# A pruned-weight matmul whose first tokens are loaded ahead of its weights

## The chip, the cores and the metric

The kernel runs on one core of one Trainium2 chip. The metric is the device time of one execution in microseconds (us), as a median over executions. Time points in the text count from the start of the profiled span.

## The reference

```python
B, S, D = 16, 512, 1024            # x: [16, 512, 1024], w: [1024, 1024], b: [1024], bf16
N, M = 2, 4
wg = w.reshape(D // M, M, D)       # groups of four rows
mag = jnp.abs(wg)
order = jnp.argsort(mag, 1)
thr = jnp.take_along_axis(mag, order[:, M - N:M - N + 1, :], 1)
wp = (wg * (mag >= thr)).reshape(D, D)
return jnp.einsum("bsd,df->bsf", x, wp) + b
```

In each column, of every four weights in successive rows only those stay whose size is at least the second largest of the four. Then 8192 tokens are multiplied with the pruned matrix and the bias is added.

## The kernel before

**Weights.** A weight tile `w_gh[(g, h)]` holds half g of the rows and half h of the columns: 128 partitions with one group of four rows each (index m), 512 columns. They are pruned in six pieces; piece 0 is rows g = 0, columns 0 to 255. `load_w` (L69, its DMA at L71) loads a piece or two of its four rows.

VectorE prunes a piece in `abs_piece` (L109) and `prep_piece` (L124). With `abs` the sizes of the four rows, it forms `hi` and `lo`, the larger and smaller of each pair of rows; t1, the smaller `hi`; t2, the larger `lo`; and the threshold `thr`, the larger of t1 and t2, which is the second largest of four. `keep` compares the sizes with it (L150), `prune` multiplies the weights with the mask, in place (L153). In piece 0 the abs step goes by pairs of rows (m = 0, 1 and m = 2, 3), `hi` too, `lo` in one instruction. Then rows 0 and 1 are kept and pruned in two column halves each, and after them rows 2 and 3.

**Tokens.** 64 tiles of 128 tokens. For tiles 0 to 7, the first half of the features is loaded as it lies (`load_x`, L76, DMA at L79), transposed by TensorE (`transpose_half`, L182, four 128 x 128 transposes a tile into a PSUM bank) and copied to `xT` by ScalarE (`copy_half`, L187). Everything else is transposed by DMA.

**Queues.** Loads are issued from SP's DMA queue (q1 in the profile) and from ScalarE's (q10). Both run on the same 16 DMA engines. On ScalarE the two loads stand ahead of its activation table load.

**Order.** `K` keeps instructions in the order in which they are written. The start is written out by hand in the list `FRONT` (L285), read token by token. W and w are fillers on TensorE: matmuls of ones into an unused bank, 512 or 128 columns wide (`warm`, L105). T.t transposes tile t, C.t copies it. A.i and P.i are `abs_piece` and `prep_piece`. N.i.t.m is the product of tile t with row m of weight piece i (L203, 256 columns), M.i.t the same for all four rows. So N.0.0.0 is TensorE's first use of pruned weights and N.0.0.2 the first of rows 2 and 3. I, D, G, Q, L issue loads, U moves pruned weights from their group layout to `wp_nat`, V and O handle partial sums; the rest of the run is a loop over token tiles (L369).

Of the kernel before, what the change touches and what calls it, by code (L numbers as in the profile page):

```python
# [10 lines left out]
def kernel(  # L11
# [7 lines left out]
    nc = tc.nc  # L19
    P = 128  # L20
    bf16 = mybir.dt.bfloat16
    fp32 = mybir.dt.float32
    u16 = mybir.dt.uint16
    Alu = mybir.AluOpType
    Act = mybir.ActivationFunctionType
    K = tc.keep_in_program_order

    B, S, D = x.shape
# [10 lines left out]
    T, F = 8, 6  # L39
# [25 lines left out]
    def w_of(i):  # L65
        g, c0, c1 = pieces[i]
        return w_gh[(g, c0 // FH)][:, :, c0 % FH:c0 % FH + c1 - c0]

    def load_w(g, c0, c1, eng=nc.sync, m0=0, m1=4):  # L69
        dst = w_gh[(g, c0 // FH)][:, m0:m1, c0 % FH:c0 % FH + c1 - c0]  # L70
        K(eng.dma_start(dst, wv[:, g, m0:m1, c0:c1]))  # L71
# [4 lines left out]
    def load_x(ta, tb, eng=nc.sync):  # L76
        xt = const.tile([P, tb - ta, KH], bf16, name=f"xh_{ta}")
        src = xf[ta * P:tb * P, 0:KH].rearrange("(t p) c -> p t c", p=P)
        K(eng.dma_start(xt[:], src))  # L79
        for t in range(ta, tb):  # L80
            xh[t] = xt[:, t - ta, :]

    load_w(0, 0, 256, nc.sync, 0, 2)
    load_w(0, 0, 256, nc.scalar, 2, 4)
    load_x(0, 2)
    load_x(2, 4, nc.scalar)
    load_x(4, 5)
    load_x(5, 6)
    load_w(0, 256, 512)
# [16 lines left out]

    mags = {}

    def abs_piece(i, on_act):  # L109
        g, c0, c1 = pieces[i]  # L110
        n = c1 - c0
        if n <= 256:
            mag = mags_pool.tile([P, 4, n], bf16, name="mag")[:]
        else:
            mag = mag2_pool.tile([P, 4, n], bf16, name="mag2")[:]
        if on_act:
            K(nc.scalar.activation(mag, w_of(i), Act.Abs))
        else:
            for ms in (slice(0, 2), slice(2, 4)) if i == 0 else (slice(0, 4),):
                K(nc.vector.tensor_single_scalar(  # L120
                    mag[:, ms].bitcast(u16), w_of(i)[:, ms].bitcast(u16), 0x7FFF, op=Alu.bitwise_and))
        mags[i] = mag

    def prep_piece(i):  # L124
        g, c0, c1 = pieces[i]
        n = c1 - c0
        mag = mags.pop(i)
        magv = mag.rearrange("p (a j) f -> p a j f", j=2)
        hi = tmp.tile([P, 2, FH], bf16, name="hi")[:, :, :n]
        lo = tmp.tile([P, 2, FH], bf16, name="lo")[:, :, :n]  # L130
        for a in ((0, 1), (1, 2)) if i == 0 else ((0, 2),):
            a = slice(*a)
            K(nc.vector.tensor_tensor(hi[:, a], magv[:, a, 0, :], magv[:, a, 1, :], op=Alu.max))
        K(nc.vector.tensor_tensor(lo, magv[:, :, 0, :], magv[:, :, 1, :], op=Alu.min))
        t1 = tmp.tile([P, FH], bf16, name="t1")[:, :n]
        t2 = tmp.tile([P, FH], bf16, name="t2")[:, :n]
        K(nc.vector.tensor_tensor(t1, hi[:, 0, :], hi[:, 1, :], op=Alu.min))
        thr = tmp.tile([P, FH], bf16, name="thr")[:, :n]
        cols = (slice(0, n // 2), slice(n // 2, n)) if i == 0 else (slice(0, n),)
        for c in cols:  # L140
            K(nc.vector.tensor_tensor(t2[:, c], lo[:, 0, c], lo[:, 1, c], op=Alu.max))
        for c in cols:
            K(nc.vector.tensor_tensor(thr[:, c], t1[:, c], t2[:, c], op=Alu.max))
        mask = tmp.tile([P, 4, FH], bf16, name="mask")[:, :, :n]

        halves = (slice(0, 2), slice(2, 4)) if i < 3 else (slice(0, 4),)

        def keep(ms, c=slice(0, n)):
            tb = thr[:, None, c].to_broadcast([P, ms.stop - ms.start, c.stop - c.start])
            K(nc.vector.tensor_tensor(mask[:, ms, c], mag[:, ms, c], tb, op=Alu.is_ge))  # L150

        def prune(ms, c=slice(0, n)):
            K(nc.vector.tensor_tensor(w_of(i)[:, ms, c], w_of(i)[:, ms, c], mask[:, ms, c], op=Alu.mult))  # L153

        if i == 0:
            for step in (keep, prune):
                for c in cols:
                    step(halves[0], c)
            keep(halves[1])
            prune(halves[1])  # L160
        else:
            for ms in halves:
                keep(ms)
            for ms in halves:
                prune(ms)
# [100 lines left out]
    def issue_batch(t0, nb):  # L266
# [16 lines left out]


    FRONT = """  # L285
        I.1.0.512 D.0 A.0 P.0 W W W W W W W W W w w T.0 T.1 C.0 T.2 T.3 C.1 w T.4 C.2 N.0.0.0 N.0.0.1 T.5
        N.0.1.0 N.0.1.1 N.0.0.2 N.0.0.3 N.0.1.2 N.0.1.3 M.0.2 A.1 C.3 P.1 U.0.0.0.512 I.1.512.1024 G C.4 C.5
        M.0.3 N.0.4.0.1 T.6 T.7 C.6 N.0.4.2.3 C.7 A.2 M.0.5 M.0.6 P.2 M.0.7 N.1.0.0.1 N.1.1.0.1 A.3
        N.1.2.0.1 N.1.0.2.3 N.1.1.2.3 N.1.2.2.3 V.0.0 M.1.3 V.0.1 M.1.4 V.0.2 M.1.5 M.1.6 V.0.3 M.1.7 V.0.4
        P.3 N.2.0.0.1 V.0.5 N.2.1.0.1 N.2.0.2.3 V.0.6 N.2.1.2.3 M.2.2 V.0.7 M.2.3 M.2.4 M.2.5 M.2.6 A.4 P.4  # L290
# [9 lines left out]
    for tok in FRONT.split():  # L300
# [6 lines left out]
        elif k in "Ww":  # L307
            warm(FH if k == "W" else P)
        elif k == "A":
            abs_piece(n[0], n[0] == 3)  # L310
        elif k == "P":
            prep_piece(n[0])
        elif k == "T":
            transpose_half(n[0])
# [89 lines left out]
```

## Time and profile before

| | |
|---|---|
| runs | median 232.98 us of 3 (232.91 to 233.33) |
| profiled execution | 232.85 us |
| its span, first to last instruction | 231.1 us |
| mean granted TensorE clock | 1.000 |
| TensorE busy | 226.7 us (98%) |
| VectorE busy | 120.2 us (52%) |
| ScalarE busy | 18.0 us (8%) |
| first weight loads, issued 0.73 us | SP: 2.6 us to landing; ScalarE: 2.8 us |
| first token loads, issued 1.25 us | SP: 3.4 us to landing; ScalarE: 3.8 us |

The profile is one execution. An engine's instructions are listed by source line, with start, duration and what ended the idle time before. A row of several instructions runs from the first one's start to the last one's end, and those of one engine may overlap by their tails, so the distance from one start to the next is what an instruction costs in a stream. "To landing" counts from the start of the issuing instruction until the data is there. The chain of waits goes back from the last instruction to whatever released each step.

### The profile page before, as it was taken

Reading aid. Unit: us, or ns where it says so; the run is one execution under the profiler, and the core shown is the slowest. Engines: PE = TensorE matmul, PEld = TensorE weight load, DVE = VectorE, ACT = ScalarE, POOL = GpSimd, SP = SyncE. Lnnn points to the kernel's source line nnn. Section 1 sums busy time; section 2 is a strip of 40 time slices with the busy share of each in tenths; the row PEclk is TensorE's granted clock in tenths of the full one; section 3 lists DMA queues with packets and bytes.
Section 4 is the critical chain, followed back from the end, with each engine's and each line's share of the span. In section 5 each row is a group of like instructions: output and inputs, shape, how many; then the busy total and the mean of one; then the engine's idle time right before and its main releaser. Section 6 shows DMA issues by size and latency. Waiting matters only on the chain.

```text
span 231.1 us, 2772 instructions
## 1 busy us (share of the span) xinstructions
PE 226.7 (98%) x1137; PEld 111.1 (48%) x1156; DVE 120.2 (52%) x213; ACT 18.0 (8%) x33; POOL 0.7 (0%) x6
## 2 busy tenths in 40 slices
PE   8999999999999999999999999999999999999995
PEld 4887444444444444444444444444444444444443
DVE  4999787867987424424424424424423423433434
ACT  3868400000000000000000000000000000000000
POOL 1000000000000000000000000000000000000000
PEclk9999999999999999999999999999999999999999
DMA  6989989999447222991249522696128950122222
GB/s 214 299 180 262 210 195 197 289 247 318 185 182 272 91 84 80 272 249 59 80 115 278 152 95 91 129 245 194 70 91 197 241 197 34 60 91 91 91 94 91
DMA packets 77228, 38.19 MB, mean 165 GB/s; under 512 B 63136, under 2 KB 69024, under 8 KB 77216
## 3 DMA queue, kind: packets, MB, share of 16 engines
q1 hardware_dynamic: 67568, 20.88, 41.4%
q10 hardware_dynamic: 9648, 17.14, 20.1%
q8 instruction: 9, 0.15, 0.3%
q14 instruction: 3, 0.02, 0.0%
HBM read 3.41 MB, written 16.78 MB: 87 GB/s over the span
## 4 chain that ended last, share of the span: by engine, by line
PE 98%; DVE 0%; issue 0%
PE bank L369 73%; PE bank L203 16%; PE bank L263 6%; PE bank L105 2%; PE bank L182 1%; DVE o_last L354 0%
## 5 line engine op out<-in xcount | busy, mean ns | idle before, releaser
L369 PE MATMUL bank<-wp_nat,xTb 128*128 128x512 bf16 x737 | 161.7, 379 | 0.8
L248 DVE TENSOR_TENSOR o_pair<-bank,bias_sb 128x512 bf16<-128x512 f32 x104 | 67.3, 687 | 99.5 <-PE bank L369 94.1
L369 PEld LDWEIGHTS <-xTb 128*128 128x128 bf16 x752 | 73.6, 98 | 88.7
L239 DVE TENSOR_TENSOR stage<-bank,stage 128x512 f32<-128x512 f32 x22 | 14.2, 687 | 4.3 <-PE bank L203 4.2
L203 PE MATMUL bank<-w,xT 128*128 128x256 bf16 x128 | 14.5, 273 | 0.0
L243 DVE TENSOR_TENSOR o_pair<-stage,bias_sb 128x512 bf16<-128x512 f32 x22 | 14.0, 684 | 0.0
L203 PE MATMUL bank<-wp_nat,xg 128*128 128x512 bf16 x62 | 13.9, 379 | 0.1
L203 PEld LDWEIGHTS <-xT 128*128 128x128 bf16 x128 | 12.3, 98 | 1.6
L235 ACT COPY stage<-bank 128x512 f32<-128x512 f32 x22 | 11.5, 613 | 4.5 <-PE bank L203 4.5
L203 PE MATMUL bank<-wp_nat,xfill 128*128 128x512 bf16 x47 | 10.6, 379 | 0.1
L263 PE MATMUL bank<-wp_nat,xfill 128*128 128x512 bf16 x47 | 10.5, 379 | 0.1
L203 PEld LDWEIGHTS <-xg 128*128 128x128 bf16 x64 | 6.3, 98 | 7.6
L263 PEld LDWEIGHTS <-xfill 128*128 128x128 bf16 x48 | 4.7, 98 | 5.7
L203 PEld LDWEIGHTS <-xfill 128*128 128x128 bf16 x48 | 4.7, 98 | 5.5
L369 PE MATMUL bank<-wp_nat,xTs 128*128 128x512 bf16 x32 | 7.1, 379 | 0.0
L150 DVE TENSOR_TENSOR mask<-mag,thr 128x512 bf16<-128x512 bf16 (+3 forms) x10 | 5.6, 584 | 0.2
L153 DVE TENSOR_TENSOR w<-w,mask 128x512 bf16<-128x512 bf16 (+3 forms) x10 | 5.6, 582 | 0.1
L105 PE MATMUL bank<-const-bfloat16-1.0 128*128 128x512 bf16 (+1 forms) x12 | 4.4, 540 | 0.8 <-PEq L388 0.8
L369 PEld LDWEIGHTS <-xTs 128*128 128x128 bf16 x32 | 3.1, 98 | 3.8
L187 ACT COPY xT<-bank 128x512 bf16<-128x512 bf16 x8 | 4.1, 605 | 2.7 <-PE bank L182 2.7
L120 DVE TENSOR_SCALAR mag<-w 128x512 uint16<-128x512 uint16 (+2 forms) x6 | 2.7, 466 | 2.5 <-DMA w<-in_w_dram 2.5
L263 PE MATMUL bank<-wp_nat,xTb 128*128 128x64 bf16 (+3 forms) x40 | 3.7, 251 | 0.0
(20 smaller groups left out, 27.1 us busy)
## 6 DMA issues: line engine op xcount, KB each, us to landing
out_dram<-o_pair ACTq DMA_DIRECT2D x25, 512.0 KB, 2.8
out_dram<-o_pair ACTq DMA_DIRECT2D x13, 256.0 KB, 2.1
wp_nat<-w SPq DMA_DIRECT2D x16, 128.0 KB, 2.9
w<-in_w_dram SPq DMA_DIRECT2D x3, 512.0 KB, 5.5
xh<-in_x_dram SPq DMA_DIRECT2D x2, 256.0 KB, 4.1
xh<-in_x_dram ACTq DMA_DIRECT2D x1, 256.0 KB, 3.8
xh<-in_x_dram SPq DMA_DIRECT2D x2, 128.0 KB, 3.6
w<-in_w_dram SPq DMA_DIRECT2D x1, 256.0 KB, 4.0
```

The lines of the kernel that those rows point to most:

```text
L105: K(nc.tensor.matmul(bank[7][:, :n], lhsT=ones[:, :P], rhs=ones[:, :n], start=True, stop=True))
L120: K(nc.vector.tensor_single_scalar(mag[:, ms].bitcast(u16), w_of(i)[:, ms].bitcast(u16), 0x7FFF, op=Alu.bitwise_and))
L150: K(nc.vector.tensor_tensor(mask[:, ms, c], mag[:, ms, c], tb, op=Alu.is_ge))
L153: K(nc.vector.tensor_tensor(w_of(i)[:, ms, c], w_of(i)[:, ms, c], mask[:, ms, c], op=Alu.mult))
L187: K(nc.scalar.copy(xt[:], src))
L203: K(nc.tensor.matmul(dst, lhsT=lhs, rhs=rhs, start=c0 == 0 and m == 0, stop=c1 == FH and m == 3))
L235: K(nc.scalar.copy(stage[(h, t)][:], bank[own[(h, t)]][:]))
L239: K(nc.vector.tensor_tensor(st, bank[own[(2 + h, t)]][:], st, op=Alu.add))
L243: K(nc.vector.tensor_tensor(get_o(t)[:, f], stage.pop((h, t))[:], bias_sb[:, f], op=Alu.add))
L248: K(nc.vector.tensor_tensor(get_o(t)[:, f], bank[bk][:], bias_sb[:, f], op=Alu.add))
L263: K(nc.tensor.matmul(bank[bk][:, :c1 - c0], lhsT=xN[t][:, kt, :], rhs=wp_nat[h][:, kt, c0:c1], start=kt == 0, stop=kt == KT - 1))
L369: K(nc.tensor.matmul(bank[bks[h]][:], lhsT=xN[t][:, kt, :], rhs=wp_nat[h][:, kt, :], start=kt == 0, stop=kt == KT - 1))
```

## The change

Three parts, all in the first 8 us.

1. The first loads are put in another order. SP's queue gets tiles 0 and 1, then 2 and 3, and 4 and on as before. ScalarE's queue gets both pairs of rows of weight piece 0, rows 0 and 1 first.
2. On VectorE, piece 0 goes by pairs of rows: abs, `hi` and `lo` of rows 0 and 1, then the same of rows 2 and 3. `lo` becomes two instructions.
3. In `FRONT`, TensorE gets seven W instead of nine, seven w instead of three, a copy behind each of the first three transposes (on ScalarE, whose own order is unchanged), and T.5 ahead of all products. The four products of rows 0 and 1 with tiles 0 and 1 thus follow each other, and then those of rows 2 and 3.

```diff
-    load_w(0, 0, 256, nc.sync, 0, 2)
+    load_x(0, 2)
+    load_w(0, 0, 256, nc.scalar, 0, 2)
+    load_x(2, 4)
     load_w(0, 0, 256, nc.scalar, 2, 4)
-    load_x(0, 2)
-    load_x(2, 4, nc.scalar)
     load_x(4, 5)
     load_x(5, 6)
     load_w(0, 256, 512)
...
+    def abs_rows(mag, i, ms):
+        K(nc.vector.tensor_single_scalar(
+            mag[:, ms].bitcast(u16), w_of(i)[:, ms].bitcast(u16), 0x7FFF, op=Alu.bitwise_and))
...
-        else:
-            for ms in (slice(0, 2), slice(2, 4)) if i == 0 else (slice(0, 4),):
-                K(nc.vector.tensor_single_scalar(
-                    mag[:, ms].bitcast(u16), w_of(i)[:, ms].bitcast(u16), 0x7FFF, op=Alu.bitwise_and))
+        elif i > 0:
+            abs_rows(mag, i, slice(0, 4))
...
-        for a in ((0, 1), (1, 2)) if i == 0 else ((0, 2),):
-            a = slice(*a)
+        for a in (0, 1) if i == 0 else (slice(0, 2),):
+            if i == 0:
+                abs_rows(mag, i, slice(2 * a, 2 * a + 2))
             K(nc.vector.tensor_tensor(hi[:, a], magv[:, a, 0, :], magv[:, a, 1, :], op=Alu.max))
-        K(nc.vector.tensor_tensor(lo, magv[:, :, 0, :], magv[:, :, 1, :], op=Alu.min))
+            K(nc.vector.tensor_tensor(lo[:, a], magv[:, a, 0, :], magv[:, a, 1, :], op=Alu.min))
...
-        I.1.0.512 D.0 A.0 P.0 W W W W W W W W W w w T.0 T.1 C.0 T.2 T.3 C.1 w T.4 C.2 N.0.0.0 N.0.0.1 T.5
-        N.0.1.0 N.0.1.1 N.0.0.2 N.0.0.3 N.0.1.2 N.0.1.3 M.0.2 A.1 C.3 P.1 U.0.0.0.512 I.1.512.1024 G C.4 C.5
+        I.1.0.512 D.0 A.0 P.0 W W W W W W W w w w T.0 C.0 T.1 C.1 w w w T.2 C.2 T.3 w T.4 T.5
+        N.0.0.0 N.0.0.1 N.0.1.0 N.0.1.1 N.0.0.2 N.0.0.3 N.0.1.2 N.0.1.3 M.0.2 A.1 C.3 P.1 U.0.0.0.512 I.1.512.1024 G C.4 C.5
```

## The prediction

> **What bounds the kernel now.** I read the chain of waits first, then the start of the run, since only the start is changed.
>
> From the page, and from the chain in order of time cut to the first 12 us (start, duration, what):
>
> ```profile
> span 231.1 us, 2772 instructions
> PE 98%; DVE 0%; issue 0%
> 0.77 4.21 PE bank L105 x11
> 4.99 1.28 PE bank L182 x16
> 6.99 1.75 PE bank L203 x16
> ```
>
> TensorE is the chain from 0.77 us to the end and never waits in between. So the time is TensorE's own list of instructions plus any new gap. At the start this list holds fillers (L105: W has 512 columns, w 128), transposes (L182) and the products with weight piece 0 (L203).
>
> What stands just behind the chain is VectorE. Its timeline (start, duration, line, operands, count, idle before):
>
> ```profile
> 3.35 0.51 DVE L120 TENSOR_SCALAR mag<-w 128x512 uint16<-128x512 uint16 x2 [2.47 <-DMA w<-in_w_dram]
> 3.77 0.49 DVE L133 TENSOR_TENSOR hi<-mag 128x256 bf16<-128x256 bf16 x2
> 4.17 0.42 DVE L134 TENSOR_TENSOR lo<-mag 128x512 bf16<-128x512 bf16 x1
> 4.51 0.29 DVE L137 TENSOR_TENSOR t<-hi 128x256 bf16<-128x256 bf16 x1
> 5.66 0.49 DVE L153 TENSOR_TENSOR w<-w,mask 128x256 bf16<-128x256 bf16 x2
> 6.52 0.43 DVE L153 TENSOR_TENSOR w<-w,mask 128x512 bf16<-128x512 bf16 x1
> ```
>
> It starts when the first weights land (3.35) and works without a gap. Rows 0 and 1 of piece 0 are pruned at 5.66 + 0.49 = 6.15, rows 2 and 3 at 6.52 + 0.43 = 6.95. TensorE needs the first at N.0.0.0 (6.38) and the second at N.0.0.2, 7.04 in the trace. So the second prune is done only 0.09 us before it is used: nearly every delay of VectorE's first piece reaches TensorE, and from there the end.
>
> Last the DMA queues, q1 (SP) and q10 (ScalarE), in two windows, 2.3 to 2.8 and 3.15 to 4.65 us (packets, MB, share of the 16 engines):
>
> ```profile
> q1 hardware_dynamic: 166, 0.08, 56.5%
> q10 hardware_dynamic: 157, 0.08, 53.0%
> ...
> q1 hardware_dynamic: 271, 0.26, 55.7%
> q10 hardware_dynamic: 272, 0.26, 49.7%
> ```
>
> The shares add up to over 100%: the engines are full, and the two queues take turns packet by packet, whatever a packet's size. A weight packet is 512 B, a token packet 1024 B. From the shares one takes 0.53 x 0.5 x 16 / 157 = 0.027 us of one engine, the other 0.497 x 1.5 x 16 / 256 = 0.046 (16 of the 272 are the 4-byte packets that end a transfer). Between 1.8 and 2.3 us only q1 runs (101 packets), though both queues issued at 0.73: ScalarE's first transfer begins half a microsecond after SP's.
>
> **TensorE's part.** Two W go (0.427 each, the spacing of their weight loads: 0.85) and four w come (0.107 each while cold: 0.43). T.0 then starts at 4.78 - 0.85 + 0.11 = 4.03. T.0 and T.1 (8 x 0.107) end at 4.89, three w at 5.21, T.2 at 5.63; about there the spacing of before halves (the first 16 transposes take 1.32 = 8 x 0.107 + 8 x 0.056). T.3, w, T.4, T.5 are 13 x 0.056 = 0.73, so N.0.0.0 could start at 6.37, as before; but T.5 (4 x 0.056 = 0.22), once inside the N group, is behind it. N.0.0.2, with N.0.0.0, N.0.0.1, N.0.1.0 and N.0.1.1 ahead of it (0.44), could start at 6.82 instead of 7.04. **Without a wait this part gains 0.22 us, and no more.** The transposes' inputs cover it: the first pair, now first on SP, has its 256 packets through by about 3.2 and lands near 3.65, before 4.03; pair 2 and 3 follows, and tiles 4 and 5 (landed at 5.4 and 5.8) keep the same bytes ahead of them. ScalarE's copies start earlier, each 0.48 after the one before, and the two that the N group needs are done by 5.9. If an input is late by up to 0.8, the wait worked out below hides it.
>
> **The weights' part.** Before, rows 0-1 led SP's queue and rows 2-3 ScalarE's; they landed 2.6 and 2.8 us after an issue at 0.73, at 3.33 and 3.54. Now both are on ScalarE's queue: rows 0-1 issued at 0.73 beginning at 2.3, rows 2-3 issued at 1.25 behind them, 512 packets in all, and each takes turns with a token packet twice its size. SP's queue has a head start of 50 packets (by bytes) to 101 (by number) of the first pair's 256, so 412 to 462 token packets of tiles 0 to 3 remain from 2.3 on, and up to 512 if tile 4 is ready to fill in. The last weight packet is through at 2.3 + (512 x 0.027 + 412 to 512 x 0.046) / 16 = 4.35 to 4.64. From last packet to landing takes 0.45 (ScalarE's token pair: last packet near 4.6, landed at 1.25 + 3.8 = 5.05). So rows 2-3 land at 4.8 to 5.1; I take 4.9. Rows 0-1: 256 pairs of 0.073 / 16 from 2.3 are 1.17, through at 3.47, landed at 3.9.
>
> The bounds are wider. Below: a 128 KB weight load again lands 2.8 after its issue, 3.53 and 4.05. Above: all of tile 4 and some of tile 5 get in between, 5.4.
>
> VectorE now does abs, hi, lo for rows 0-1 and the same for rows 2-3: six steps, each starting about 0.203 after the last (the rows at 3.35, 3.56, 3.77, 3.97, 4.17 in the trace), where five took 1.16. Splitting lo costs 0.06 and is worth it only if rows 2-3 come late. t1 starts at the later of 3.93 + 1.22 = 5.15 and 4.93 + 0.61 = 5.54, against 4.51: **1.03 late**, with 0.4 idle ahead of the second abs. After t1 nothing changes: rows 0-1 are pruned at 7.18, rows 2-3 at 7.98. TensorE stands at N.0.0.0 from 6.38 to 7.22, does four products to 7.66, waits again, and starts N.0.0.2 at 8.01 (0.04 after its releaser, as ScalarE's copy after TensorE) instead of 7.04: **+0.97 us**. Both kernels have done the same work at that point.
>
> From there the orders are equal. VectorE is 1.03 late and TensorE 0.97; the next pruned rows, piece 1, are finished 0.6 ahead of their use, so 0.06 is no new wait. SP isn't moved: its order and waits stand on transfers, except the unpack at 11.7, 1.4 us behind the prune that it needs (10.27). Its load issues from 4.1 on wait for the first loads' landings, and those at 3.65, 3.9 and about 4.9 come before the issues at 4.10, 4.71 and 5.38 that reuse their semaphores. ScalarE issues two DMAs ahead of its table load, as before. Nothing later gives the 0.97 back, as TensorE has no idle time to shorten. Sum against the profiled execution (231.1 span, 232.85 in all): **232.85 + 0.97 = 233.8**. The median of the runs shown is 232.98, 0.13 above it, which the upper end of the range allows for.
>
> **The rivals.**
> 1. *The weights aren't held up* (no change): the token packets leave them room, and they land 2.8 after their issues. t1 is then at 3.56 + 1.22 = 4.78, 0.27 late, of which 0.06 is covered: +0.21, 233.06. Were rows 0-1 as early as the 3.33 that the lead place gave, it would be +0.01, 232.86; were both earlier still, by 0.3, TensorE's floor of -0.22 would be the end, 232.63 (0.03 of the 0.16). For it: 0.5 us more of lead for tokens. Against it: engines full from 2.3 on, and taking turns by packet. It decides if rows 2-3 land before 4.39 and rows 0-1 before 3.8. 0.16 in all. The Trainium skill, page "DMA: Bandwidth & Descriptors", section "Anatomy of one DMA — SWDGE (gpsimd) path", fits a transfer, on GpSimd's path, as about 2.0 us and its bytes at 436 GB/s; an estimate from it is 2.3 us for 128 KB, weights at 3.03 and 3.55, and that floor. This trace has 2.6 and 2.8 for the same size on SP's and ScalarE's queues, with the engines less full.
> 2. *Held up further*: tiles 4 and 5 share too, or the second issue on ScalarE's queue starts late (its token pair began only near 3.2); landing at 5.2 to 5.4 gives +1.28 to +1.48, 234.1 to 234.3. 0.12.
> 3. *TensorE falls back to half speed* in the new gaps (0.84 and 0.35 us), as slow as it is up to 5.6. If it stays so as long as at the start (0.77 to 5.6, 4.8 us), half of that is lost: +2.4 on top, 236.2. No row has an idle TensorE after 0.8 us, so the profile speaks neither way. 0.02. The Trainium skill, "TensorE: Matmul & The Clock Gate", section "HAM oscillation — how this bites in real kernels", wants over about 3.4 us of idleness for that; no run here shows it.
> 4. *Full speed comes sooner*, and the weights too: each transpose or filler between 4.0 and 5.6 saves 0.05, at most 0.7 for all, but VectorE must then be ready before 6.4, and no transfer row speaks for that. Beyond 0.2% faster, 232.3: 0.04.
>
> **The numbers.** 0.2% of the time is 0.47 us, about what a measurement of this kernel can tell from no change. The forecast (rows 2-3 landing between 4.4 and 5.15) has 0.66. Slower is 0.66 + 0.12 + 0.02 = 0.80, the same 0.16, faster 0.04. The likeliest landing gives 233.8. The range goes from 233.0, which takes in the better part of the first rival, to 234.4, the second with the 0.13 of the median; outside lie rivals 3 and 4 and the lucky end of the first, about 0.13.
>
> **What would show it.** Right: VectorE waits twice for weights, to about 3.9 and then 0.4 us to about 4.9; t1 near 5.5; a row of TensorE waiting for VectorE's w, about 1.2 us in two pieces, ahead of N.0.0.0 and N.0.0.2; VectorE on the chain at the start. The queue windows show weight and token packets in equal numbers from 2.3 on. Wrong: rows 2-3 landed by 4.1 (the share), N.0.0.2 at 7.0 or earlier, or a wait of TensorE elsewhere, at a transpose or past 8 us; or an end that moves by another amount than N.0.0.2 does.

## The result, and the profile after

The changed kernel takes 234.81 us (median of 6 runs, 234.75 to 234.93); the kernel before, run beside it, 233.16 (6 runs, 232.81 to 233.45). The ratio is 1.0072, 95% interval [1.0059, 1.0085]: 1.65 us slower. Its profiled execution is at 234.81 too, with a span of 233.0. The profiled execution of before, 232.85, is near the fast end of that kernel's runs, so between the two profiles the difference is 1.96 in time and 1.9 in span. Two kernels further down, e1_loads and f2_onequeue, have one run each that is some 1.5 and 1.9 us longer than their others (236.45 and 236.57, granted clock 0.993 and 0.992), which lifts their ratios and widens the intervals, so their medians say more.

The page's span and chain, and pieces of the chain in order of time (start, duration, what):

```profile
span 233.0 us, 2796 instructions
PE 95%; DMA 2%; DVE 2%; ACTq 0%; issue 0%
...
1.27 4.43 DMA w<-in_w_dram
...
8.47 0.44 DVE w L156
...
8.95 1.69 PE bank L206 x14
```

Where TensorE was the chain from 0.77 us on, it now joins at 8.95. Before that stands the load of weight rows 2 and 3: issued at 1.27, landed at 5.70. Then comes VectorE's first piece.

The waits (waiter, releaser: total, times, longest):

```profile
DVE mag L110 <- DMA w<-in_w_dram: 4.0, 2, 3.6
PE bank L206 <- DVE w L156: 1.4, 2, 1.2
PE bank L185 <- DMA xh<-in_x_dram: 0.6, 2, 0.4
```

VectorE waits for weights twice instead of once, 4.0 us instead of 2.5. TensorE has a new row, two waits for pruned weights. The third row, transposes that wait for tokens, was to be empty by the prediction.

VectorE's timeline:

```profile
4.52 0.29 DVE L110 TENSOR_SCALAR mag<-w 128x512 uint16<-128x512 uint16 x1 [3.64 <-DMA w<-in_w_dram]
5.72 0.30 DVE L110 TENSOR_SCALAR mag<-w 128x512 uint16<-128x512 uint16 x1 [0.39 <-DMA w<-in_w_dram]
6.47 0.28 DVE L140 TENSOR_TENSOR t<-hi 128x256 bf16<-128x256 bf16 x1
7.61 0.49 DVE L156 TENSOR_TENSOR w<-w,mask 128x256 bf16<-128x256 bf16 x2
8.47 0.43 DVE L156 TENSOR_TENSOR w<-w,mask 128x512 bf16<-128x512 bf16 x1
```

Weight rows 0-1 are there at 4.5 and rows 2-3 at 5.7, where 3.9 and 4.9 were forecast. From t1 to the last prune it takes 6.47 to 8.90, 2.43, as before (4.51 to 6.95).

The queues from 2.3 to 2.8 us:

```profile
DMA packets 70, 0.06 MB, mean 127 GB/s; under 512 B 0, under 2 KB 70, under 8 KB 70
...
q1 hardware_dynamic: 54, 0.06, 41.0%
q10 hardware_dynamic: 16, 0.01, 5.6%
```

The same window in the kernel before:

```profile
DMA packets 323, 0.16 MB, mean 319 GB/s; under 512 B 12, under 2 KB 323, under 8 KB 323
```

Here is what the prediction did not see. In the kernel before this half microsecond carried 323 packets, 319 GB/s, and the engines were full. Now there are 70 packets, 127 GB/s, and the engines are more than half idle. In what follows, this is called the slow start.

From 3.3 to 5.15 us, when the engines are full again, the queues of the changed kernel read:

```profile
q1 hardware_dynamic: 465, 0.44, 67.5%
q10 hardware_dynamic: 477, 0.23, 42.0%
```

Packets go in nearly equal numbers, and since a token packet is twice the size of a weight packet, the weights get a third of the bytes.

### The profile page after: what moved, and what is told of

Its sections match the earlier page's. It is cut to its first block, busy times and chain, and to the rows that moved or that the text cites. A ratio compares the mean times of both kernels' runs of the same rounds, so it can differ in the third digit from the quotient of the medians.

```text
span 233.0 us, 2796 instructions
## 1 busy us (share of the span) xinstructions
PE 227.6 (98%) x1158; PEld 110.7 (48%) x1158; DVE 120.6 (52%) x214; ACT 18.1 (8%) x33; POOL 0.7 (0%) x6
## 4 chain that ended last, share of the span: by engine, by line
PE 95%; DMA 2%; DVE 2%; ACTq 0%; issue 0%
PE bank L372 73%; PE bank L206 16%; PE bank L266 6%; DMA w<-in_w_dram 2%; DVE o_last L357 0%; DVE w L156 0%; DVE mask L153 0%; ACTq L71 0%; PE bank L185 0%; DVE mag L110 0%; DVE hi L136 0%; DVE thr L146 0%; DVE t L144 0%; DVE t L140 0%; DVE lo L137 0%
## 5 line engine op out<-in xcount | busy, mean ns | idle before, releaser
L105 PE MATMUL bank<-const-bfloat16-1.0 128*128 128x512 bf16 (+1 forms) x14 | 3.9, 432 | 0.8 <-PEq L391 0.8
```

The lines of the kernel that those rows point to most:

```text
L105: K(nc.tensor.matmul(bank[7][:, :n], lhsT=ones[:, :P], rhs=ones[:, :n], start=True, stop=True))
```

## The experiments

Theory: the order of the loads is the whole loss; VectorE and the new list on TensorE cost nothing by themselves. Within it, the landing is late because packets take turns (as forecast) and because of a slow start that the forecast didn't have. Rivals: the lists carry a part of the loss; the slow start belongs to the token tensor, to the packet size, to the load's shape, or to two queues starting together.

N.0.0.2 below is the start of the first product with weight rows 2 and 3, from the trace. Landings are those of weight rows 0-1 / 2-3, when the last of each load is in. GB/s is what the engines moved from 2.3 to 2.8 us. All of these but the median are of one profiled execution. That of f1_pertile is the slowest of its four runs (234.17 to 234.72), that of e7_tok512 the fastest of its eight (233.95 to 234.98).

| kernel | landings | GB/s | N.0.0.2 | span | median |
|---|---|---|---|---|---|
| before | 3.32 / 3.54 | 319 | 7.04 | 231.1 | 233.16 |
| after | 4.49 / 5.70 | 127 | 8.95 | 233.0 | 234.81 |
| e1_loads | 4.46 / 5.66 | 151 | 9.11 | 233.1 | 234.93 |
| e2_rest | 3.55 / 3.77 | 284 | 7.53 | 231.6 | 233.23 |
| e3_swap | 4.05 / 4.97 | 157 | 8.22 | 232.2 | 233.88 |
| e4_w1k | 4.17 / 5.74 | 225 | 9.01 | 233.2 | 234.95 |
| e5_wdata | 4.43 / 5.65 | 187 | 8.89 | 232.9 | 234.74 |
| e6_pmaj | 2.95 / 4.61 | 258 | 7.86 | 231.9 | 233.72 |
| e7_tok512 | 3.88 / 4.72 | 206 | 7.96 | 232.2 | 234.31 |
| e8_alone | 4.36 / 5.61 | 270 | 8.86 | 232.9 | 234.71 |
| f1_pertile | 3.63 / 4.59 | 271 | 7.83 | 232.9 | 234.39 |
| f2_onequeue | 3.92 / 5.49 | 342 | 8.73 | 232.8 | 234.62 |
| f3_w1kboth | 4.98 / 6.50 | 166 | 9.74 | 233.9 | 235.67 |

Span minus N.0.0.2 lies between 223.98 and 224.24 in every row but f1_pertile (225.07): what happens up to N.0.0.2 goes to the end one for one, to within 0.3 us.

**The loads alone (e1_loads).** The kernel before with this edit:

```diff
-    load_w(0, 0, 256, nc.sync, 0, 2)
+    load_x(0, 2)
+    load_w(0, 0, 256, nc.scalar, 0, 2)
+    load_x(2, 4)
     load_w(0, 0, 256, nc.scalar, 2, 4)
-    load_x(0, 2)
-    load_x(2, 4, nc.scalar)
```

> The kernel before with the new order of the loads alone (VectorE and FRONT as before). Theory A, the loads are the whole loss: rows 0-1 and 2-3 land near 4.5 and 5.7 us as in the changed kernel, t1 starts about 0.2 later than there (6.65, since hi and lo of rows 0-1 are no longer done while rows 2-3 are awaited), N.0.0.2 near 9.1 to 9.2, and the time is 1.0 to 1.3% above the kernel before with nine W, or at least as slow as the changed kernel. Theory B, the lists of TensorE and VectorE carry a good part of the loss: the time is under half of the changed kernel's loss, below 234.0.

234.93 us, ratio 1.0095 [1.0063, 1.0126], by the medians 1.0076; N.0.0.2 at 9.11. The same landings as in the changed kernel (within 0.04) and, by the medians, the same loss: theory A. The 0.16 by which N.0.0.2 comes later than there is what VectorE by pairs of rows earns once rows 2-3 are late.

**Everything but the loads (e2_rest).** The changed kernel with the loads of before (the diff above, reversed).

> The changed kernel with the loads of the kernel before (so only VectorE by pairs of rows and the new list on TensorE). Theory A: within 0.15 us of the kernel before; VectorE ends the prune of rows 2-3 near 7.0 to 7.1 (six steps instead of five), TensorE waits for the first token pair (landed 4.7) before T.0, and N.0.0.2 starts at 7.0 to 7.1 against 7.04. Theory B: at least 0.5 us slower.

233.23 us, ratio 1.0005 [0.9995, 1.0015]: 0.09 above the kernel before by the medians, theory A. The interval reaches up to 0.35 us, so a small cost of the lists isn't excluded, and the profile shows one: N.0.0.2 is at 7.53 in this profile and not at 7.0 to 7.1, partly because the same loads landed 0.23 later than in the profile of before, a difference between two executions. VectorE's steps show the rest:

```profile
3.57 0.29 DVE L110 TENSOR_SCALAR mag<-w 128x512 uint16<-128x512 uint16 x1 [2.70 <-DMA w<-in_w_dram]
4.32 0.28 DVE L110 TENSOR_SCALAR mag<-w 128x512 uint16<-128x512 uint16 x1
```

abs, hi and lo of a pair take 0.75 from start to start, where 0.61 was reckoned. Before, the abs of one pair filled the time until the other's result was ready; now hi stands right behind its own abs, and starts 0.33 after it instead of 0.21.

**The queues exchanged (e3_swap).**

```diff
-    load_x(0, 2)
-    load_w(0, 0, 256, nc.scalar, 0, 2)
-    load_x(2, 4)
-    load_w(0, 0, 256, nc.scalar, 2, 4)
+    load_x(0, 2, nc.scalar)
+    load_w(0, 0, 256, nc.sync, 0, 2)
+    load_x(2, 4, nc.scalar)
+    load_w(0, 0, 256, nc.sync, 2, 4)
```

> The changed kernel with the two queues exchanged: weights on SP's queue, tokens on ScalarE's. Theory S (the slow start belongs to tokens being served first): weights start at 1.8, the engines move about 320 GB/s from 2.3 to 2.8 as in the kernel before, rows 0-1 land near 3.4 and rows 2-3 near 4.6; N.0.0.2 near 7.7, time near 233.8. Theory R (no slow start by order, only the sharing by packets and the second place in the queue): the same 127 GB/s from 2.3 to 2.8 or rows 2-3 landing after 5.3, N.0.0.2 after 8.4.

233.88 us, ratio 1.0031 [1.0018, 1.0044]. A miss for both: the weights gain by starting first (rows 2-3 at 4.97), but the start is slow all the same, 157 GB/s. So tokens going first isn't its cause. The time is where theory S had it (near 233.8).

**Another load first (e4_w1k).**

```diff
+    load_w(1, 0, 512, nc.sync, 0, 2)
     load_x(0, 2)
...
     load_w(0, 512, 1024)
+    load_w(1, 0, 512, nc.sync, 2, 4)
...
-        I.1.0.512 D.0 A.0 P.0 W W W W W W W w w w T.0 C.0 T.1 C.1 w w w T.2 C.2 T.3 w T.4 T.5
+        D.0 A.0 P.0 W W W W W W W w w w T.0 C.0 T.1 C.1 w w w T.2 C.2 T.3 w T.4 T.5
```

> The changed kernel with one more load ahead on SP's queue: rows 0-1 of the second half's weight block, 256 KB in 1024 B packets (taken out of its later load). Time is of no interest; the window 2.3 to 2.8 us is. If tokens as data (their place in memory) make the slow start, the engines move over 280 GB/s there. If a transfer with 1024 B packets, whatever it reads, beside the ScalarE queue's weights makes it, they move under 180 GB/s as in the changed kernel (127).

234.95 us (one run). 225 GB/s, between the two expectations: inconclusive. From 2.05 to 2.3 it moved 301 GB/s. From 2.3 to 3.1 and from 2.8 to 3.05:

```profile
DMA packets 203, 0.16 MB, mean 200 GB/s; under 512 B 0, under 2 KB 203, under 8 KB 203
...
DMA packets 46, 0.04 MB, mean 143 GB/s; under 512 B 0, under 2 KB 46, under 8 KB 46
```

Up to 3.1 there is no packet under 512 B, and so none of the 4-byte packets that end a transfer: the first load on SP's queue was still running and the token load hadn't begun. The engines fell to 143 GB/s with weights alone on both queues. This load takes two rows to a partition that lie next to each other in `w`, so a slow stretch doesn't need tokens, nor rows that lie far apart.

**Tokens read from the weights' tensor (e5_wdata).**

```diff
-        src = xf[ta * P:tb * P, 0:KH].rearrange("(t p) c -> p t c", p=P)
+        src = (w if ta < 4 else xf)[ta * P:tb * P, 0:KH].rearrange("(t p) c -> p t c", p=P)
```

> The changed kernel, with the tokens of tiles 0 to 3 read from the first 512 rows of w instead of x, in the same shapes and order: the same packets from another tensor, so the product of those tiles is of other data. Theory M (the first reads of the token tensor are slow in memory): the window 2.3 to 2.8 us moves over 250 GB/s, rows 0-1 land before 4.0 and rows 2-3 before 5.2, time at or below 234.3. Theory P (the packets' pattern or their making is slow, whichever tensor): 127 GB/s again, 4.5 and 5.7, 234.8.

234.74 us, ratio 1.0070 [1.0048, 1.0093]: landings as in the changed kernel, within 0.06 (187 GB/s). Which tensor is read makes no difference to the landings; theory M falls.

**Adjacent token rows (e6_pmaj).**

```diff
-        src = xf[ta * P:tb * P, 0:KH].rearrange("(t p) c -> p t c", p=P)
+        src = xf[ta * P:tb * P, 0:KH].rearrange("(p t) c -> p t c" if ta < 4 else "(t p) c -> p t c", p=P)
```

> The changed kernel, with tiles 0 to 3 loaded so that a partition takes two adjacent token rows instead of two rows 128 apart (the same bytes of x, tokens of a pair in another order). Theory M: slow again, about 127 GB/s in the window 2.3 to 2.8 us and landings of the weights at 4.5 and 5.7. Theory P: over 250 GB/s, weights before 4.0 and 5.2.

233.72 us, ratio 1.0027 [1.0016, 1.0038]; 258 GB/s: theory P by the numbers that it named. The run isn't a clean one, so it doesn't show that the rows' distance is the cause. ScalarE's queue began first here (170 packets from 1.8 to 2.3 us, SP's none), which in no other run with tokens on SP happened, and rows 0-1 landed at 2.95.

**Smaller token packets (e7_tok512).**

```diff
-        K(eng.dma_start(xt[:], src))
+        for c in (slice(0, KH // 2), slice(KH // 2, KH)) if ta < 4 else (slice(0, KH),):
+            K(eng.dma_start(xt[:, :, c], src[:, :, c]))
```

> The changed kernel, with the loads of tiles 0 to 3 cut into two column halves each (512 B packets, two more issues on SP's queue). By the turn-taking of packets the weights' 512 packets now go against 512 packets of half the size: 512 x (0.027 + 0.027) / 16 = 1.73 us in place of 2.05 to 2.33, so without a slow start rows 2-3 land 0.3 to 0.6 before the forecast, near 4.4; with the slow start of the changed kernel (0.5 us) near 5.1. If turns are taken by bytes and not by packets, rows 2-3 land at 5.6 to 5.8 as in the changed kernel.

234.31 us, ratio 1.0058 [1.0043, 1.0073]. Rows 2-3 land at 4.72, 1.0 before those of the changed kernel, though the same bytes stand in both queues: turns go by packets, not by bytes. It lies between the two landings that turns by packets gave (4.4 without a slow start, 5.1 with). From 2.3 to 2.8 and from 2.8 to 3.3 us:

```profile
q1 hardware_dynamic: 122, 0.06, 43.4%
q10 hardware_dynamic: 91, 0.04, 33.9%
...
q10 hardware_dynamic: 184, 0.09, 61.6%
q1 hardware_dynamic: 166, 0.08, 52.9%
```

In the second window packets are near one to one, and so now are bytes. The Trainium skill, page "DMA: Bandwidth & Descriptors", section "Queues, rings and completion order", says that an engine goes round its queues a packet at a time, typically 9 to 17 descriptors to a packet. The near equal numbers agree with such turns; how long one turn is, these windows don't show. N.0.0.2 gains 0.99, of which the profile at 233.95 keeps 0.86; other runs of this kernel reach 234.98, so its median gains only 0.5.

**The weights issued later (e8_alone).**

```diff
-    load_w(0, 0, 256, nc.scalar, 0, 2)
-    load_w(0, 0, 256, nc.scalar, 2, 4)
...
     K(nc.scalar.copy(act_first[:], zeros[:]))
+    load_w(0, 0, 256, nc.scalar, 0, 2)
+    load_w(0, 0, 256, nc.scalar, 2, 4)
```

> The changed kernel, with the two weight loads issued behind ScalarE's table load (about 3.3 us), so that the tokens run alone up to then. Time is lost by this, some 1.5 us or more; the windows 1.8 to 3.3 us are what is looked at. If the slow start belongs to the token reads themselves, the engines move well under 200 GB/s from 2.3 to 2.8 with no weights beside them. If it needs both queues (tokens beside weights), tokens alone reach over 300 GB/s there.

234.71 us (one run). The edit didn't do what was meant: ScalarE issued the weights at 0.91, beside its table load, only 0.17 later. It still tells something. From 2.3 to 2.8, with only 16 weight packets among 148, the engines moved 270 GB/s, less than the 300 that theory had for tokens alone; in the next half microsecond, with both queues, 123. So the slow stretch comes here when the second queue joins. In the changed kernel SP's queue was slow before that: ScalarE's first packet came at 2.48, and from 2.05 to 2.3 the engines moved 106 GB/s.

**Tiles one by one (f1_pertile).**

```diff
-    load_x(0, 2)
+    load_x(0, 1)
+    load_x(1, 2)
     load_w(0, 0, 256, nc.scalar, 0, 2)
-    load_x(2, 4)
+    load_x(2, 3)
+    load_x(3, 4)
     load_w(0, 0, 256, nc.scalar, 2, 4)
```

> The changed kernel, with tiles 0 to 3 loaded one by one (four loads of 128 KB, one row a partition, in place of two loads with two rows 128 apart). If the slow start comes from the two far rows in one load, the engines move over 250 GB/s from 2.3 to 2.8 us and the weights land before 4.0 and 5.2. If it comes from 1024 B token packets of SP's queue beside 512 B weight packets on the other, whatever the load's shape, it stays under 180 GB/s, with landings near 4.5 and 5.7 and 234.8.

234.39 us, ratio 1.0059 [1.0039, 1.0078]. 271 GB/s, rows 0-1 and 2-3 at 3.63 and 4.59, N.0.0.2 at 7.83: with one row to a partition the slow start is gone. Each load is also half as large here, so the run doesn't tell the rows from the size. The time gains less, for a new reason. A piece of its chain and two rows of TensorE, weight loads and products:

```profile
5.01 7.51 DMA w<-in_w_dram
...
9.61 0.48 PEld L187 LDWEIGHTS <-xh 128*128 128x128 bf16 x8 [0.37 <-DMA xh<-in_x_dram]
...
15.68 1.59 PE L208 MATMUL bank<-w,xT 128*128 128x256 bf16 x13 [0.38 <-DVE w L158]
```

SP issues two loads more, and its later ones go out later: the weight load for a later piece at 5.01 instead of 4.51, and it lands at 12.52 instead of 11.10; tiles 6 and 7 land at 9.57. Of the 1.12 won at the start, counted against the changed kernel's products, 0.26 is lost at the transposes of tile 6 (9.62) and 0.57 up to the products with the late weights (15.68), the rest later.

**One queue (f2_onequeue).**

```diff
-    load_w(0, 0, 256, nc.scalar, 0, 2)
+    load_w(0, 0, 256, nc.sync, 0, 2)
     load_x(2, 4)
-    load_w(0, 0, 256, nc.scalar, 2, 4)
+    load_w(0, 0, 256, nc.sync, 2, 4)
```

> The changed kernel with all four loads on SP's queue, in the same order (pair 0-1, weight rows 0-1, pair 2-3, weight rows 2-3). If the slow start needs two queues that start at once, the one queue runs at 250 GB/s or more from 2.3 us; without turns, weight rows 0-1 have 393 KB up to their end and land near 3.9, rows 2-3 have 786 KB and land near 4.9 to 5.1, time 233.8 to 234.0. If the token load is slow by itself, the window stays under 180 GB/s and rows 2-3 land after 5.4.

234.62 us, ratio 1.0096 [1.0017, 1.0174], by the medians 1.0067. The window from 2.3 to 2.8 us:

```profile
q1 hardware_dynamic: 188, 0.17, 100.2%
```

The same token load as in the changed kernel, now 342 GB/s: alone it isn't slow. Rows 0-1 land at 3.92 as expected. Rows 2-3 land at 5.49, a miss by 0.4 to 0.6, and the time misses its 233.8 to 234.0 with them: later the one queue moves less (223 GB/s from 3.3 to 3.8) than two together, and it issues every 0.5 us.

**Equal packets (f3_w1kboth).**

```diff
-    load_w(0, 0, 256, nc.scalar, 0, 2)
+    load_w(0, 0, 512, nc.scalar, 0, 2)
     load_x(2, 4)
-    load_w(0, 0, 256, nc.scalar, 2, 4)
+    load_w(0, 0, 512, nc.scalar, 2, 4)
...
-    load_w(0, 256, 512)
```

> The changed kernel, with ScalarE's two weight loads made 512 columns wide (1024 B packets, 256 KB each; SP's later load of columns 256 to 511 falls away). Both queues then carry 1024 B packets. If unequal packet sizes make the slow start, the engines move over 250 GB/s from 2.3 to 2.8 us. If not, under 180. Rows 2-3 land later in any case (more bytes ahead), near 5.5 without and 6 with a slow start; the time is of no interest.

235.67 us (one run), 166 GB/s: unequal sizes alone aren't the cause.

Taken together, from 2.3 to 2.8 us the engines are slow when the first load on one queue takes two token rows 128 apart to a partition and a load begins on the other (after, e1, e3, e5, e7, f3: 127 to 206 GB/s). They are not with one queue (342), nor with single rows in loads of half the size (271), nor with two loads of 512 B weight packets (319, 284). With adjacent rows it is 258 in e6_pmaj, where the queues began in the other order, and 225 in e4_w1k, falling to 143. So that both queues take part is shown; which property of the load does it, the rows' distance, their number or the load's size, is not. It also belongs to the start: in the kernel before, token loads of the same shape begin at about 2.8 behind the weights, and the engines move 348 GB/s from 2.8 to 3.3. What the engines wait for, the making of descriptors or the memory, is open: some are idle in the changed kernel, and packets run long besides (its 1024 B packets that began before 2.9 took 0.075 us on the mean, those of f2_onequeue 0.051).

## Why the prediction was right or wrong

*Direction and mechanism: right.* The weights land later, VectorE starts later, TensorE waits ahead of N.0.0.0 and N.0.0.2, the loss goes to the end one for one, and no wait is added behind N.0.0.2. TensorE's own gain is hidden behind the new wait.

*Size: wrong by a factor of two.* N.0.0.2 moved by 1.91 instead of 0.97, and 234.81 lies above the 234.4 at which the range ended. The terms that were mis-sized:

1. *The landing of rows 2-3, 5.70 instead of 4.9: 0.80.* The sum let the engines be full from 2.3 on, since they were so in the kernel before. By 3.3 us they had moved 0.04 + 0.06 + 0.12 = 0.22 MB; before, it was 0.38. At 0.34 MB a microsecond that is some 0.4 to 0.5 us; it is the step that failed, a rate taken over from a row in which other loads ran. The runs had 127 GB/s there instead of 319; what causes it stays open. Then tile 4 took turns as well, which was the second rival: up to 5.15 us SP's queue had 654 packets through, 544 of them tiles 0 to 3 and their ends. The 110 others are 0.3 us. The last weight packet was through at 5.15, not 4.45, and landing took 0.55 after it, not 0.45. (0.5 and 0.3 add up to more than 0.70, as the rate was a little higher afterwards: 324 to 378 GB/s from 3.3 to 5.3. The split is an estimate: in f1_pertile, without the slow start, rows 2-3 landed at 4.59, ahead of the forecast.)
2. *VectorE's steps: 0.13.* abs, hi, lo in a row cost 0.75 a pair, not 0.61. Independent instructions between a result and its use had hidden that, and the sum took their spacing for dependent ones.

0.97 + 0.80 + 0.13 = 1.90. The range ended at 5.4 for the landing, which came at 5.70. The lower bound, 2.8 us after the issue, was beside the point: it became 3.75 and 4.43.

*Turns by packet: right, but not from the lines shown.* In both windows that the prediction read, the two queues carried packets of one size (512 B in the first, 1024 B in the second), so equal numbers there couldn't tell turns by packet from turns by byte. The changed kernel from 3.3 on and e7_tok512 do. From 2.3 to 2.8, where equal numbers were forecast as well, it was 54 to 16.

*The tokens land later too:* 4.31 for the first pair instead of 3.65, so T.0 waits until 4.36, and T.2 to 5.54. By the prediction a delay of up to 0.8 would be hidden behind TensorE's wait for weights, and it was: N.0.0.0 waits until 8.15 in any case. A wait at a transpose was one of the prediction's signs of being wrong; it came (0.6 us) and cost nothing.

*SP was moved.* By the prediction its issue at 4.10 had the landings that it waits for behind it. With rows 0-1 landing at 4.49 it went out at 4.51 instead. Here no wait of TensorE came of that, by luck: in f1_pertile, with SP's issues later still, one did.

*Rivals.* The first (weights not held up) fell: rows 0-1 landed at 4.49 and rows 2-3 at 5.70, where it needed 3.8 and 4.39. The second was half right, for tile 4. The fourth came true in its first half: full speed came early. The first eight transposes, and the products after the wait:

```profile
4.36 0.48 PEld L185 LDWEIGHTS <-xh 128*128 128x128 bf16 x8 [0.40 <-DMA xh<-in_x_dram]
...
8.15 0.42 PEld L206 LDWEIGHTS <-xT 128*128 128x128 bf16 x4 [1.32 <-issue]
```

Eight weight loads in 0.48 are some 0.055 apart: full speed from 4.36 at the latest, not 5.6. (The three fillers ahead, at 3.71, 3.82 and 3.91, put the step at about 3.9. The granted clock in the profile's rows is 1.00 on both sides of it, so the spacing is what tells.) It bought nothing, since TensorE only waits longer. The third rival fell: after 1.2 us of waiting the four products still follow 0.11 apart. The Trainium skill, "TensorE: Matmul & The Clock Gate", section "Part 1: The HAM clock gate", has the window free-running, so that the step to full speed shifts by 0.5 us either way. The traces spread wider: the spacing halves at about 3.9 in the changed kernel, 4.4 in e1_loads, 5.6 in the kernel before and 5.9 in f1_pertile, with TensorE at work from 0.77 us in all four.

## What to carry to other kernels

When loads are put in another order, the rate at which they start isn't the one that the old order had: take it as unknown between a third of the full rate and the full one (127 to 342 GB/s here), and let the range say so. Two queues share the DMA engines by packets, so the load with small packets loses beside one with large packets; where a small-packet load is what the next engine waits for, it goes first on both queues, as in the kernel before. An instruction that uses the result just ahead of it costs more than its spacing in an interleaved stream (0.33 us from start to start instead of 0.21).

## What the runs showed of the hardware that was not expected

Two loads of 256 packets each, on the two queues and issued at the same time, ran at 127 GB/s from 2.3 to 2.8 us when one of them took two token rows 128 apart to a partition; the same token load on one queue with the weights ran at 342. From 3.3 to 5.3 us the changed kernel was at 324 and over. And the queue that starts first isn't fixed by the issue: where both issues stand at 0.73, SP's led by 0.3 to 0.7 us in every run but one, and ScalarE's by 0.5 in e6_pmaj.
